# RWKV-7 recurrence into hash-routed MoE: decays of the later rounds turned on chip by VectorE, batches paired 0-2 and 1-3, and a new order of PE steps

## The chip, the cores and the metric

The kernel runs on one core of a Trainium2 chip. The metric is the device time of one execution in microseconds (us). A profile gives the span, from the first to the last instruction of one profiled execution, and the same execution's own time, which is a little longer than its span.

## What is computed

The reference is an RWKV-7 recurrence over `(batch 4, heads 8, sequence 768, head size 40)` in float32, whose output feeds a mixture of experts:

```
for t in range(S):
    y[:, :, t] = einsum('bhd,bhde->bhe', rt, state)
    Sa = einsum('bhde,bhe->bhd', state, at)
    state_decay = state * wt[:, :, None, :] - einsum('bhd,bhe->bhde', Sa, bt)
    state = state_decay + einsum('bhd,bhe->bhde', vt, kt)
x = y as (3072 tokens, 320)
out[token] = relu(x[token] @ w1[e]) @ w2[e],   e = hash of token_ids, 8 experts, F = 1024
```

## The kernel before

**Chunks, tiles, rounds.** The recurrence is computed in chunks of C = 64 steps. A tile `u` (0 to 23) is one chunk `n = u // 2` of one pair of batches `g = u % 2`: batches 0 and 1, or 2 and 3, one in partitions 0 to 63 and one in 64 to 127. The decays `w` are prepared for two chunks and all four batches at a time, in a round `ri` (0 to 5), so a round serves four tiles. A round makes `p`, which multiplies `a` (and later the output rows), and `q`, which multiplies `b` and `k`.

**Stages of a round (`decays`).** Load `w` as (batch-head, half chunk) rows; clamp (L265, VectorE); 14 chain products `prefix` and `suffix` (L270, L285; VectorE for rounds 0 and 1, GpSimd after); `own` (L275 to L277, VectorE) and, in the same step, the exchange of ends between the two halves of a chunk by eight small matmuls into `ex_ps` (L278 to L281); `ends` and the reciprocal (L290 to L300); `spread` over the rows (L304; GpSimd 2.9 us each after round 0); and then a turn from (batch-head, time) rows to (time, batch-head) rows. Round 0 turns by VectorE's transpose of 32 by 32 blocks (`turned`, L309) into borrowed space. Rounds 1 to 5 turn through DRAM: `store` (L324) scatters `p` and `q` in pieces of 40 floats, and each tile loads its slices `pl` and `ql` back (L408, L410).

**Stages of a tile.** `tile_a`: load `a`, `b`, `k` (L236, L397), multiply by `p` and `q` (L414; GpSimd after the first four tiles), turn `a` and `z = (b, k)` by TensorE (`at_t`, `z_t`), then the step `a`, a matrix of all products, of which ScalarE and VectorE copy the parts `no`, `pk` and `mk`. Four tiles make a group, whose 32 by 32 triangular blocks VectorE inverts together (`group_i`: transpose `nb`, 31 pairs of products L516 and L519, transposes `ut` and `ug`). `tile_m` completes the inverse from `ut` and `ug` (steps `x` and `u`). `tile_s` loads `r` and `v` and turns them (`rv`); `tile_b` runs the recurrence of the tile (steps `r0`, `r1`, `c`, `rcc`, `nc`, `rcv`, `s`, `y`, `sd`) and writes 128 rows of output to DRAM (`xs` L689, L692).

**What sets the order.** Every step is entered into a plan with a due time in ticks; the plan is sorted, and the engines get their instructions in exactly this order (L855 to L857). `STEPS` (L128) gives the place of a step within a tick. Tile `u` does its part of `tile_b` at tick `u + LAG`, LAG = 8. So ticks 8 to 23 hold the recurrence of one tile and `tile_a` of the tile eight later, ticks 24 to 31 the recurrence alone, and before tick 8 only `tile_a` and the first inversions run. `order` breaks ties: decays (8) and inversions (9) come behind steps of the same time. SyncE's queue issues nearly all loads and stores, in the plan's order; GpSimd's queue issues `py` and the output rows. An instruction that waits holds up everything behind it on its engine or queue.

**Buffers that the change meets.** PSUM: `psa` and `psb`, two buffers each, taken in turn. `z_all` has NZ = 11 slots. `xi`, `um`, `xs`, `py` have one buffer.

After the recurrence all its SBUF is freed, weights are loaded, and the experts run one after another (L935 on).

The changed order of steps touches these lines:

```
STEPS = ["c", "z", "rcc", "nc", "rcv", "s", "a", "y", "x", "sd", "r0", "at_t", "u", "r1", "rv"]
decays(2, -5.5, 0.45, (0.5, 2.5), 6.41, 6.43, 6.5, 6.6)
    decays(ri, t - 5.8, t - 5.3, (t - 5.2, t - 3.9), t - 3.75, t - 3.6, t - 3.55, t - 3.2)
    group_i(gi, 3.43, 3.47, 6.4)
    group_i(gi, t0 + 0.05, t0 + 0.1, t0 + 3.1)
```

Of the kernel before, what the change touches and what calls it, by code (L numbers as in the profile page):

```python
# [8 lines left out]
F32 = mybir.dt.float32  # L9
# [9 lines left out]
def kernel(  # L19
# [108 lines left out]
    STEPS = ["c", "z", "rcc", "nc", "rcv", "s", "a", "y", "x", "sd", "r0", "at_t", "u", "r1", "rv"]  # L128
# [21 lines left out]
    NZ = LAG + 3  # L150
    z_all = hold.tile([P, NZ, 2, HP, P], F32, name="z_all")
    for lo, hi, when in ((0, 4, -9.0), (4, LAG, -3.0), (LAG, NZ, 0.3)):
        @at_tick(when)
        def _(lo=lo, hi=hi):
            nc.gpsimd.memset(z_all[:, lo:hi].rearrange("p i b hp (two x) -> p (i b hp two) x", two=2)[:, :, D:C], 0.0)

    def z_r(u):
# [7 lines left out]
    lent = [x_all[:].rearrange("p i b hp x -> p (i b hp x)"),  # L165
            z_all[:, LAG:LAG + 3].rearrange("p i b hp x -> p (i b hp x)")]

    @at_tick(0.35)
    def _():
        nc.gpsimd.memset(x_all[:].rearrange("p i b hp (two x) -> p (i b hp two) x", two=2)[:, :, D:C], 0.0)  # L170
# [23 lines left out]
    pq_dram = [[nc.dram_tensor(f"{n}_rows{i}", (RN * C, B * H, D), F32) for n in "pq"] for i in range(NR)]  # L194
# [38 lines left out]
    def load(eng, dst, src, b0, t0):  # L233

        for be in range(2):
            eng.dma_start(per_head(dst[half(be)]),  # L236
                          src[b0 + be, :, t0:t0 + C, :].rearrange("h t e -> t h e"))
# [11 lines left out]
    def decays(ri, t_load, t_clamp, t_chain, t_own, t_ends, t_spread, t_store):  # L249
# [5 lines left out]
        @at_tick(t_load)  # L255
        def _():
            x["pb"] = pb = work.tile([P, HC * D], F32, tag="pb", name="pb")
            x["qb"] = work.tile([P, (HC + 1) * D], F32, tag="qb", name="qb")
            for y in range(2 * RN):
                src = w.rearrange("b h (n t) e -> (b h) n (t e)", t=HC)[:, ri * 2 * RN + y]  # L260
                eng = nc.scalar if fast and y % 2 else nc.sync
                eng.dma_start(pb[y * BH:(y + 1) * BH], src)
# [9 lines left out]
        def own():  # L272
            p, q = segs(x["pb"]), segs(x["qb"])
            x["own"] = own = work.tile([P, SEG, D], F32, tag="own", name="own", bufs=1)
            nc.vector.tensor_tensor(own[:], p[:, :, SL - 1], q[:, :, SL - 1], op=OP.mult)  # L275
            for s in range(SEG - 2, -1, -1):
                nc.vector.tensor_tensor(own[:, s], own[:, s], own[:, s + 1], op=OP.mult)  # L277
            x["ex"] = ex = bank([P, D], "ex_ps")  # L278
            for y in range(2 * RN):
                mm(ex[y * BH:(y + 1) * BH], ident[:, (y | 1) * BH:((y | 1) + 1) * BH],  # L280
                   ones[:, 0:D] if y % 2 else own[:, 0])  # L281
# [24 lines left out]
        def turned(i, src):  # L306
            lo, hi = (lent[i][:, j * BH * D:(j + 1) * BH * D] for j in range(2))
            x["qp"[i]] = lo, hi
            nc.vector.transpose(lo.rearrange("p (c e) -> p e c", e=D), src.rearrange("p (t e) -> p e t", e=D))  # L309
            nc.scalar.copy(hi[half(1)], lo[half(1)])  # L310
            if i == 0:
                nc.scalar.copy(lo[half(1)], lo[half(0)])
                nc.scalar.copy(hi[half(0)], hi[half(1)])
            else:
                lo, hi = (t.rearrange("p (g be x) -> p g be x", be=2, x=DM) for t in (lo, hi))
                nc.scalar.copy(hi[half(0), :, 1], lo[half(1), :, 0])
                nc.scalar.copy(lo[half(1), :, 0], lo[half(0), :, 1])
                for j in range(RN):
                    nc.sync.dma_start(pq_dram[ri][0][half(j)].rearrange("t bh e -> t (bh e)"), x["p"][j][half(j)])

        def store(i):
            src = (x["pb"][:], x["qb"][:, D:])[i]
            for y in range(2 * RN):
                nc.sync.dma_start(pq_dram[ri][i][y * HC:(y + 1) * HC].rearrange("t bh e -> bh t e"),  # L324
                                  src[y * BH:(y + 1) * BH].rearrange("p (t e) -> p t e", e=D))
# [6 lines left out]
        def spread_all():  # L332
            if fast:
                spread(nc.vector, x["qb"][:], x["ends"][:, 1:])
                turned(0, x["qb"][:, D:])
                recip()
                spread(nc.vector, x["pb"][:], x["own"][:])
                turned(1, x["pb"][:])
            else:
                spread(nc.gpsimd, x["pb"][:], x["own"][:])  # L340
                spread(nc.gpsimd, x["qb"][:], x["ends"][:, 1:])
# [6 lines left out]
        at_tick(t_ends, order=8)(ends_and_recip)  # L348
        at_tick(t_spread, order=8)(spread_all)
        if not fast:  # L350
            for i in range(2):
                at_tick(t_store + 0.25 * i, order=8)(lambda i=i: store(i))

        @at_tick(t_ends + 0.5, order=8)
        def _():
            p = bank([P, P], "en_ps")
            nc.tensor.transpose(p[0:R, :], e2_r(ri)[:], ident[:])
            x["pend"] = t = work.tile([P, RN, B, HP], F32, tag="pend", name="pend", bufs=5)
            for par in range(2):
                rows = half(par)  # L360
                nc.scalar.copy(t[rows].rearrange("p n b h -> p n (b h)"),
                               p[rows].rearrange("p (n y c two) -> p n y c two", n=RN, y=2, two=2)[:, :, 0, :, par])

    def of_batches(rows, b0, n):
        return rows[:, b0 * H:(b0 + n) * H, :].rearrange("t bh e -> t (bh e)")

    def tile_a(u):
# [8 lines left out]
        if early:  # L376
            t_in, t_pq, t_mul = -8.9 + 0.01 * u, None, -6.0 + 0.01 * u
            t_mulz = -6.1 + 0.01 * u if u < 2 else t_mul - 0.005
            t_z, t_at, t_a = u - 0.3, (-0.15, 0.5, 0.95, 1.0)[u], u + 0.9 if u < 3 else u + 0.4
        elif second:  # L380
            base = 4 + 0.7 * (u - 4)
            t_in, t_pq, t_mul = (0.55, 0.97, 0.2, 1.05)[u - 4], 3.1 + 0.05 * (u - 4), base - 0.5
            t_mulz = t_mul
            t_z, t_at, t_a = base - 0.3, base - 0.15, base + 0.4
        else:
            t_in, t_pq, t_mul = u - 2.3, max(u - 2.4, 6.9 + 0.02 * (u - 8)), max(u - 1.7, 7.0)
            t_mulz = t_mul
# [3 lines left out]
        def _():  # L391
            x["z"] = z_r(u)
            x["at"] = r1_r(u // GRP) if u in (3, 7) else at_r(u)
            load(eng, x["at"][:], a, 2 * g, n * C)
            for be in range(2):
                for src, rows in ((b, half(be)), (k, half(1 - be))):
                    eng.dma_start(per_head(x["z"][rows, be]),  # L397
                                  src[2 * g + be, :, n * C:(n + 1) * C, :].rearrange("h t e -> t h e"))

        if not early:  # L400
            @at_tick(t_pq)
            def _():
                pl = work.tile([P, DM], F32, tag="pl", name="pl")
                ql = work.tile([P, 2, DM], F32, tag="ql", name="ql")
                x["p"], x["q"] = pl[:], [ql[:, be] for be in range(2)]
                p_rows, q_rows = (d[rn * C:(rn + 1) * C] for d in pq_dram[ri])
                for be in range(2):
                    eng.dma_start(pl[half(be)], of_batches(p_rows, 2 * g + be, 1))  # L408
                for i in range(2):
                    eng.dma_start(ql[half(i)], of_batches(q_rows, 2 * g, 2))  # L410
# [4 lines left out]

        @at_tick(t_mulz)
        def _():
            eng = nc.vector if early else nc.gpsimd
            if early:
                q = rounds[0]["q"][rn]  # L420
                x["q"] = [q[:, (2 * g + be) * DM:(2 * g + be + 1) * DM] for be in range(2)]
            for be in range(2):
                times(eng, x["z"][:, be], x["q"][be])

        @at_tick(t_mul)
        def _():
            if early:
                p = rounds[0]["p"][rn]
                x["p"] = p[:, (2 * g + rn) * DM:(2 * g + rn + 1) * DM]
            times(nc.vector if early else nc.gpsimd, x["at"][:], x["p"])  # L430
# [25 lines left out]
        def _():  # L456
# [11 lines left out]
            x["no"] = no = work.tile([P, 2, HP, BLK], F32, tag="no", name="no", bufs=LAG)  # L468
            nc.scalar.copy(pk, pb[..., 0:BLK])
# [10 lines left out]
            nc.scalar.copy(no[:], pb[..., BLK:])  # L480

# [52 lines left out]
    def tile_m(u, t0):  # L534
# [4 lines left out]
        @at_tick(t0 - 1, "x")  # L539
# [24 lines left out]
    def tile_s(u, t0):  # L564
# [6 lines left out]
        def _():  # L571
            x["r"], x["x"] = r_r(u), x_all[:, u % 3]
            load(nc.sync, x["r"][:], r, 2 * g, n * C)
            for be in range(2):
                nc.sync.dma_start(per_head(x["x"][half(1 - be), be]),
                                  v[2 * g + be, :, n * C:(n + 1) * C, :].rearrange("h t e -> t h e"))

        @at_tick(t0 - 0.3)
        def _():
            x["py"] = py = work.tile([P, DM], F32, tag="py", name="py", bufs=1)  # L580
            for be in range(2):
                nc.gpsimd.dma_start(py[half(be)], of_batches(pq_dram[ri][0][rn * C:(rn + 1) * C], 2 * g + be, 1))
# [13 lines left out]
    def tile_b(u, t0):  # L596
# [61 lines left out]
        if not last:  # L658
            @at_tick(t0, "s")
            def _():  # L660
# [9 lines left out]
                pend = rounds[ri]["pend"][0:R, rn, 2 * g:2 * g + 2]  # L670
# [6 lines left out]
        def _():  # L677
# [12 lines left out]
            for be in range(2):  # L690
                r0 = (2 * g + be) * S + n * C
# [15 lines left out]
    decays(0, -9.0, -8.0, (-7.9, -7.6), -7.7, -7.4, -7.2, None)  # L707
    decays(1, -8.5, 0.1, (0.15, 1.85), 1.88, 2.2, 2.65, 2.7)
    decays(2, -5.5, 0.45, (0.5, 2.5), 6.41, 6.43, 6.5, 6.6)
    for ri in range(3, NR):  # L710
        t = ri * RN * NG
        decays(ri, t - 5.8, t - 5.3, (t - 5.2, t - 3.9), t - 3.75, t - 3.6, t - 3.55, t - 3.2)
# [5 lines left out]
    for gi in range(NU // GRP):  # L718
# [3 lines left out]
        else:  # L722
            group_i(gi, t0 + 0.05, t0 + 0.1, t0 + 3.1)
# [362 lines left out]
```

## Time and profile before

| | |
|---|---|
| median of 3 runs | 781.4 us (777.3 to 785.85) |
| profiled execution, its own time | 782.22 us |
| its span | 780.4 us |
| mean granted TensorE clock | 0.874 |
| TensorE busy | 623.9 us, 80% of the span |
| VectorE busy | 337.1 us, 43% |
| ScalarE busy | 278.5 us, 36% |
| GpSimd busy | 253.8 us, 33% |
| DMA packets | 201886, of them 177518 under 512 B |
| DMA traffic | 83.31 MB |

A row of instructions in the profile gives line, engine, operation, output and inputs, shape, count, then busy time and the mean of one in ns, then the engine's idle time ahead of them and what ended it. In a timeline a row begins with start and duration in us, and a bracket gives the idle time before it and the releaser. The clock is the share of full speed that TensorE was granted. `PEld` is the loading of weights into TensorE, which overlaps its matmuls.

### The profile page before, as it was taken

Reading aid. Unit: us, or ns where it says so; the run is one execution under the profiler, and the core shown is the slowest. Engines: PE = TensorE matmul, PEld = TensorE weight load, DVE = VectorE, ACT = ScalarE, POOL = GpSimd, SP = SyncE. Lnnn points to the kernel's source line nnn. Section 1 sums busy time; section 2 is a strip of 40 time slices with the busy share of each in tenths; the row PEclk is TensorE's granted clock in tenths of the full one; section 3 lists DMA queues with packets and bytes.
Section 4 is the critical chain, followed back from the end, with each engine's and each line's share of the span. In section 5 each row is a group of like instructions: output and inputs, shape, how many; then the busy total and the mean of one; then the engine's idle time right before and its main releaser. Section 6 shows DMA issues by size and latency. Waiting matters only on the chain.

```text
span 780.4 us, 24437 instructions
## 1 busy us (share of the span) xinstructions
PE 623.9 (80%) x10686; PEld 468.4 (60%) x10686; DVE 337.1 (43%) x713; ACT 278.5 (36%) x614; POOL 253.8 (33%) x336
## 2 busy tenths in 40 slices
PE   0343607899789898999989889189999999999993
PEld 0342506788668777888778778146465565565652
DVE  6849802667684656465658512111711102102100
ACT  0642502467455655665665554011101111101110
POOL 3253536525453755433323122221230212310100
PEclk9965555699886979997999999669899999999997
DMA  9567375577477659774435232696532162320000
GB/s 168 111 111 152 60 143 113 93 152 138 79 141 139 99 87 131 132 122 54 49 47 67 54 63 45 217 348 221 165 108 85 42 221 59 100 85 8 26 3 28
DMA packets 201886, 83.31 MB, mean 107 GB/s; under 512 B 177518, under 2 KB 192367, under 8 KB 201776
## 3 DMA queue, kind: packets, MB, share of 16 engines
q1 hardware_dynamic: 189008, 64.32, 38.8%
q0 software_dynamic: 6336, 16.08, 9.3%
q10 hardware_dynamic: 6432, 1.31, 1.0%
q8 instruction: 85, 1.39, 0.7%
q14 instruction: 25, 0.20, 0.1%
HBM read 66.56 MB, written 15.44 MB: 105 GB/s over the span
## 4 chain that ended last, share of the span: by engine, by line
PE 62%; issue 8%; DVE 6%; ACT 6%; DMA 3%; POOL 2%; SPq 2%; POOLq 0%; ACTq 0%; DVEq 0%
PE dn_ps L921 12%; PE up_ps L901 10%; PE r_ps L220 6%; PE s_ps L220 6%; PE y_ps L220 4%; PE rc_ps L220 4%; PE u_ps L220 3%; PE t_ps L485 3%; PE up_ps L897 3%; PE a_ps L220 3%; PE sd_ps L701 2%; PE z_ps L452 2%; PE nc_ps L654 2%; ACT rt L592 2%; DMA xg<-x_rows,src_all 1%
## 5 line engine op out<-in xcount | busy, mean ns | idle before, releaser
L921 PE MATMUL dn_ps<-w,ht 128*128 128x320 f32 x384 | 104.9, 433 | 0.0
L901 PE MATMUL up_ps<-xt,w 128*128 128x416 f32 x256 | 97.7, 536 | 0.0
L921 PEld LDWEIGHTS dn_ps<-w,ht 128*128 128x128 f32 x384 | 72.8, 190 | 32.1 <-issue 1.9
L911 POOL DMA_INDIRECT out_dram<-o,idx_all x26 | 25.7, 987 | 190.4 <-ACT o L910 185.5
L901 PEld LDWEIGHTS up_ps<-xt,w 128*128 128x128 f32 x256 | 49.2, 197 | 48.6 <-issue 48.6
L692 POOL DMA_DIRECT2D x_rows<-xs x48 | 26.3, 554 | 159.4 <-DVE xs L689 83.3
L519 DVE TENSOR_TENSOR ub<-ub,outer 128x31 f32<-128x31 f32 (+15 forms) x186 | 65.0, 349 | 6.4
L645 DVE TENSOR_TENSOR mr<-rc_ps,after 128x1024 f32<-128x1024 f32 x24 | 29.4, 1224 | 86.1 <-PE rc_ps L220 86.1
L516 DVE TENSOR_TENSOR outer<-ub,nb 128x31 f32<-128x31 f32 (+15 forms) x186 | 63.0, 338 | 4.8 <-ACT ub L501 0.2
L904 DVE TENSOR_SCALAR ht<-up_ps 128x416 f32<-128x416 f32 x32 | 18.9, 591 | 96.9 <-PE up_ps L901 96.9
L886 DVE COPY xt<-xg_ps 128x384 f32<-128x384 f32 x24 | 12.1, 552 | 101.7 <-PE xg_ps L885 101.7
L452 PE MATMUL z_ps<-ident,z_all 64*128 64x64 f32 x384 | 32.0, 277 | 29.9 <-POOL z_all L414 14.1
L452 PEld LDWEIGHTS z_ps<-ident,z_all 64*128 64x128 f32 x384 | 27.9, 180 | 33.4 <-POOL z_all L414 14.6
L414 POOL TENSOR_TENSOR z_all<-z_all,ql 128x320 f32<-128x320 f32 x40 | 33.9, 864 | 40.0 <-DMA ql<-q_rows 22.1
L910 ACT COPY o<-dn_ps 128x320 f32<-128x320 f32 x24 | 10.2, 426 | 101.6 <-PE dn_ps L921 101.6
L220 PE MATMUL rc_ps<-rt,cv 64*64 64x64 f32 x1536 | 38.1, 245 | 9.4 <-ACT cv L628 8.9
L220 PEld LDWEIGHTS rc_ps<-rt,cv 64*64 64x64 f32 x1536 | 31.1, 153 | 15.9 <-ACT cv L628 10.0
L674 ACT COPY st<-sc 40x320 f32<-40x320 f32 x44 | 20.1, 457 | 57.0 <-DVE sc L671 56.7
L906 ACT ACTIVATE ht<-up_ps 128x416 f32<-128x416 f32 x32 | 16.0, 515 | 66.3 <-PE up_ps L901 66.2
L880 POOL DMA_INDIRECT xg<-x_rows,src_all x26 | 27.2, 1044 | 30.5 <-PE xg_ps L885 15.8
L897 PE MATMUL up_ps<-xt,w 64*128 64x416 f32 x128 | 29.7, 566 | 7.1 <-DVE xt L886 3.2
L220 PE MATMUL a_ps<-at_t,z_t 64*64 64x64 f32 x1408 | 32.2, 251 | 3.6 <-ACT at_t L438 2.6
(189 smaller groups left out, 1168.0 us busy)
## 6 DMA issues: line engine op xcount, KB each, us to landing
w<-in_moe_w_dram SPq DMA_DIRECT2D x8, 1280.0 KB
w<-in_moe_w_dram SPq DMA_DIRECT2D x8, 1024.0 KB
ql<-q_rows SPq DMA_DIRECT2D x40, 160.0 KB
r<-in_r_dram SPq DMA_DIRECT2D x48, 80.0 KB
x_all<-in_v_dram SPq DMA_DIRECT2D x48, 80.0 KB
py<-p_rows POOLq DMA_DIRECT2D x48, 80.0 KB, 4.4
x_rows<-xs POOLq DMA_DIRECT2D x48, 80.0 KB, 2.6
wt<-in_w_dram SPq DMA_DIRECT2D x6, 640.0 KB
```

The source lines that it names most:

```text
L220: nc.tensor.matmul(out_, lhsT=lhsT, rhs=rhs, start=start, stop=stop, skip_group_check=True)
L414: eng.tensor_tensor(t, t, by.rearrange("p (h e) -> p h e", e=D), op=OP.mult)
L452: nc.tensor.transpose(p[:, i, c0:c0 + C], x["z"][half(i), be, hp, :], ident[half(i), half(i)])
L516: nc.vector.tensor_tensor(tv, ub[:, 0:j + 1, j:j + 1].to_broadcast([P, j + 1, m]), nb[:, j, j + 1:].unsqueeze(1).to_broadcast([P, j + 1, m ...
L519: nc.vector.tensor_tensor(o, o, tv, op=OP.add)
L645: nc.vector.tensor_tensor(t[:].rearrange("p two h t -> p (two h) t"), p[:].rearrange("p two (h t) -> p (two h) t", t=C), after[:].unsqueez ...
L692: nc.gpsimd.dma_start(x_rows[r0:r0 + C, :], xs[half(be)])
L880: nc.gpsimd.indirect_dma_start(out=xg[:, 0:DM], out_offset=None, in_=x_rows[:], in_offset=bass.IndirectOffsetOnAxis(ap=idx, axis=0))
L897: nc.tensor.matmul(banks[-1][:], lhsT=w1[rows, w:w + P], rhs=xt[rows, 2, 0:n], start=True, stop=False)
L901: nc.tensor.matmul(p[:], lhsT=w1[:, c * F + f * P:c * F + (f + 1) * P], rhs=xt[:, c, 0:n], start=False, stop=(c == 1))
L911: st = nc.gpsimd.indirect_dma_start(out=out[:], out_offset=bass.IndirectOffsetOnAxis(ap=idx, axis=0), in_=o[:], in_offset=None, bounds_che ...
L921: nc.tensor.matmul(p[:], lhsT=ht[:, f, j * P:(j + 1) * P], rhs=w2[:, f, :], start=(f == 0), stop=(f == FP - 1))
```

## The change

- Rounds 2 to 5 are turned by VectorE's transpose, `p` and `q`, into SBUF (`pt`, and `qt`, one buffer each). `p` goes to DRAM in one contiguous store for the later `py`; the upper and lower halves of `q` are put in place by three DMAs from SBUF to SBUF. Round 1 still goes through DRAM, but is loaded back for all its tiles at once. The per-tile loads `pl` and `ql` are gone; the multiplications read `pt` and `qt`.
- Batches are paired 0 with 2 and 1 with 3. With the rows of `w` loaded in another order (16 rows to a DMA), a turned round then has both batches of a pair in the right halves; `p` needs no copies between halves, in round 0 either.
- Round 2's `own`, exchange, `ends` and `spread` come at 3.38 to 3.5, ahead of the first inversion, and not at 6.41 to 6.5 behind it. Round 2 is turned at 6.45.
- In rounds 3 to 5 the exchange comes half a tick behind `own`, and the transpose `en_ps` a tick behind that.
- Step `u` goes between `c` and `rcc`; `z` goes from there to between `rcv` and `s`; `x` goes one tick earlier. Inversions are due sooner (`t0 + 2.85`, not `t0 + 3.1`, behind a step `a` that is itself 0.07 tick later).
- `b` and `k` are loaded at `u - 1.42` and multiplied at `u - 0.6` (before: `u - 2.3` and `u - 1.7`), `a` multiplied at `u - 0.9`; `z_all` has 10 slots. `no` is copied ahead of `pk`.

```diff
-    STEPS = ["c", "z", "rcc", "nc", "rcv", "s", "a", "y", "x", "sd", "r0", "at_t", "u", "r1", "rv"]
+    STEPS = ["c", "u", "rcc", "nc", "rcv", "z", "s", "a", "y", "x", "sd", "r0", "at_t", "r1", "rv"]
...
-    NZ = LAG + 3
+    NZ = LAG + 2
...
+    def batch(g, be):
+
+        return be * NG + g
...
+        def turned(i, dst):
+            src = x["qb"][:, D:] if i else x["pb"][:]
+            nc.vector.transpose(dst.rearrange("p (c e) -> p e c", e=D), src.rearrange("p (t e) -> p e t", e=D))
+
+        def turn_p():
+            x["p"] = pt = work.tile([P, BH * D], F32, tag="pt", name="pt", bufs=1)
+            if ri != 1:
+                turned(0, pt[:])
+                nc.sync.dma_start(p_dram[ri][:].rearrange("t c e -> t (c e)"), pt[:])
             else:
+                nc.sync.dma_start(pt[:], p_dram[ri][:].rearrange("t c e -> t (c e)"))
+
+        def turn_q():
+            x["q"] = qt = work.tile([P, 2, BH * D], F32, tag="qt", name="qt", bufs=1)
+            if ri == 1:
+                for i in range(2):
+                    nc.sync.dma_start(qt[half(i)], q_dram[:].rearrange("(be t) c e -> t be (c e)", be=2))
+                return
+            turned(1, qt[:, 0])
+            copy = nc.scalar.copy if fast else nc.sync.dma_start
+            copy(qt[half(1), 1], qt[half(1), 0])
+            copy(qt[half(0), 1], qt[half(1), 0])
+            copy(qt[half(1), 0], qt[half(0), 0])
...
-            t_in, t_pq, t_mul = u - 2.3, max(u - 2.4, 6.9 + 0.02 * (u - 8)), max(u - 1.7, 7.0)
-            t_mulz = t_mul
+            t_in, t_inz, t_mul, t_mulz = u - 2.3, u - 1.42, u - 0.9, u - 0.6
...
-                for be in range(2):
-                    eng.dma_start(pl[half(be)], of_batches(p_rows, 2 * g + be, 1))
-                for i in range(2):
-                    eng.dma_start(ql[half(i)], of_batches(q_rows, 2 * g, 2))
...
-        @at_tick(t0 - 1, "x")
+        @at_tick(t0 - 2, "x")
...
-    decays(2, -5.5, 0.45, (0.5, 2.5), 6.41, 6.43, 6.5, 6.6)
+    decays(2, -5.5, 0.45, (0.5, 2.5), 3.38, 3.41, 4.0, 3.5, (6.45, 6.46))
...
-        decays(ri, t - 5.8, t - 5.3, (t - 5.2, t - 3.9), t - 3.75, t - 3.6, t - 3.55, t - 3.2)
+        decays(ri, t - 5.8, t - 5.3, (t - 5.2, t - 3.9), t - 3.75, t - 3.17, t - 2.17, t - 3.1, (t - 1.57, t - 1.44))
...
-            group_i(gi, t0 + 0.05, t0 + 0.1, t0 + 3.1)
+            group_i(gi, t0 + 0.03, t0 + 0.06, t0 + 2.85)
```

In the new signature of `decays` the times are those of load, clamp, chain, `own`, exchange, `en_ps`, `spread` and the two turns.

## The prediction

> **What bounds the kernel now.** I read busy time and clock by stretch first (start and end in us, busy time of each engine, clock, DMA share, GB/s):
>
> ```profile
> 0.00:117.00 117.00, 37.22 (x779) 32.68 (x779) 76.00 (x160) 39.87 (x85) 48.18 (x67) 0.69 0.67 124
> 117.00:409.00 292.00, 259.81 (x6700) 222.35 (x6701) 175.29 (x383) 163.17 (x353) 134.52 (x183) 0.86 0.62 105
> 409.00:494.00 85.00, 75.32 (x2232) 65.52 (x2230) 37.20 (x76) 42.63 (x93) 17.22 (x33) 1.00 0.32 55
> 494.00:780.40 286.40, 251.55 (x976) 147.85 (x976) 48.58 (x96) 32.85 (x84) 53.86 (x54) 0.93 0.36 117
> ```
>
> Four stages: a prologue in which TensorE works 37 of 117 us; ticks 8 to 24, TensorE 89% busy at a clock of 0.86; the last ticks at full clock; the experts (286 us), whose instructions the change leaves alone. Next, how the prologue ends, in the timelines of TensorE, VectorE and GpSimd and the chain of what ended last:
>
> ```profile
> 117.11 0.70 PE L485 MATMUL t_ps<-ident,at 64*128 64x64 f32 x8 [21.45 <-POOL at L414]
> 132.88 0.27 PE L220 MATMUL ex_ps<-own,ident 128*32 128x40 f32 x1 [5.38 <-DVE own L277]
> ...
> 58.48 1.98 DVE L507 STREAM_TRANSPOSE nb<-pk 128x1024 f32<-128x1024 f32 x1
> 87.60 0.31 DVE L275 TENSOR_TENSOR own<-pb,qb 128x160 f32<-128x160 f32 x1
> 129.39 0.24 DVE L743 TENSOR_SCALAR eid<-tok 128x24 int32<-128x24 int32 x1 [30.42 <-DMA tok<-in_moe_token_ids_dram]
> ...
> 95.05 2.89 POOL L304 TENSOR_TENSOR pb<-pb,own 128x1280 f32<-128x1280 f32 x1
> 114.57 1.67 POOL L414 TENSOR_TENSOR z_all<-z_all,ql 128x320 f32<-128x320 f32 x2 [11.83 <-DMA ql<-q_rows]
> ...
> 111.53 2.91 DMA ql<-q_rows
> ```
>
> TensorE stands 21.45 us before the first tick: round 2's `own` comes only behind the first inversion (87.6), then `spread` (95.05), stores, loads (landed 114.4), the multiplication. Then it stands 5.38 us more, since the exchange needs round 3's `own`, which stands in VectorE's queue behind `eid`, which waits for token ids queued in SyncE's queue behind those transfers. Last, what a steady tick is made of, and what stops it:
>
> ```profile
> 442.93 0.69 PE L220 MATMUL rc_ps<-rt,cv 64*64 64x64 f32 x32 [1.08 <-ACT cv L628]
> 182.76 1.01 PE L452 MATMUL z_ps<-ident,z_all 64*128 64x64 f32 x16 [0.54 <-ACT cv L593]
> 202.00 0.27 PE L220 MATMUL ex_ps<-own,ident 128*32 128x40 f32 x1 [2.41 <-DVE own L277]
> 211.56 0.69 PE L220 MATMUL x_ps<-ut,no 32*32 32x32 f32 x32 [1.40 <-DVE ends L292]
> 227.44 1.13 PE L220 MATMUL y_ps<-z_all,mr 128*64 128x40 f32 x32 [2.39 <-DVE mr L645]
> 303.72 0.37 PE L220 MATMUL y_ps<-z_all,mr 128*64 128x40 f32 x6 [2.04 <-issue]
> ```
>
> `mr` (L645) marks the ticks: tick 8 at 134.38, tick 9 at 157.04, 10 at 171.59, 11 at 185.68, ... 24 at 408.77, 25 at 420.81. An undisturbed early tick is 14.09 us, a late one 12.05. Ticks 9 to 24 take 274.4, against 16 x 14.09 = 225.4: 49 us lie in waits of 1.4 to 2.4 us and in the lower clock after them.
>
> **The change part by part.** *Prologue.* Round 2's `own`, `ends`, reciprocal now precede the inversion: 1.95 + 0.32 + 1.15 + 0.24 = 3.7 us of VectorE (rows at 87.60 to 92.3). Against that, `a` of tile 1 stood 4 us behind round 1's exchange (3.99 idle at 44.5, for `own`) and no longer does; I let these cancel, so the inversion again ends near 87.6 (a bound from either side: 83 to 92). VectorE then turns `p` and `q`. Round 0's rows are the same instruction:
>
> ```profile
> 17.55 2.71 DVE L309 STREAM_TRANSPOSE x_all<-qb 128x1280 f32<-128x1280 f32 x1
> ```
>
> So `pt` is there at 90.3. But the tiles 4 to 7, one each 5.6 us (copies `pk` at 74.70, 80.27, 85.83, 91.97), are not faster: round 1 still goes through DRAM, its 2 x 2.9 us of `spread` for round 2 now stands between their multiplications, and GpSimd's last `mk` ends near 95.1 as now. Then its queue holds a memset and four chain products (0.2 + 4 x 0.53) and the multiplication of `a` (0.86): 98.4. TensorE's turn of tile 8's `a` moves from 117.1 to 98.4. From there to `rcv`'s end: 0.70 + 1.86 + 1.14, 1.1 of ScalarE's copies, then c 1.1, u 1.85, 1.06, 1.04, 1.06 (half-clock rows of 117 to 134) = 10.9, so 109.3. `mr` waits longer: SyncE's queue issues the `pt` store, two `q` copies, a third when they have landed (near 97), `b`, `k` and `a` of tiles 8 to 10 (10.5), `r` and `v` (2.6), then the token ids at 108, landed 2.4 later; `eid`, `mine`, three pairs, `own`: 114.4. Tick 8: 134.4 - 114.4 = **20 us gained**. The exchange half a tick behind `own` takes the 5.38 wait away; it is in these 20.
>
> *The pipeline.* `u` (1.05) now covers ScalarE's copies between `c` and `rcc`, `z` between `rcv` and `s`: the 0.54 goes, a tick becomes 13.55, and 16 of them 216.8. The price is on VectorE. In every fourth tick the order behind `mr` is `ut`, `ug`, `sc`, `pt`, `mk`, `xs` (and `qt`). From the end of `rcv`: mr 1.14, two transposes to 4.75, sc 5.2, pt 7.8, mk 8.4, xs 8.85. TensorE does z 1.0, s 1.8, a 1.1, y 1.5, x 0.6, sd 1.0, and `r0` at 7.0 must wait until `xs` has emptied the bank: 1.85, in three ticks (10, 14, 18) = 5.6. The step `x` a tick earlier takes most of the slack that `ut` had (VectorE needs 21.4 for the pairs, 2.1 for nb, 5.2 for two ticks' small work, 4.1 for own and ends, 2.3 per tick of waiting, in 37.5 us): late by 0 to 4 us, I take 2, for four groups = 8. Tick 9 starts cold, 4; routing work at tick 13 as now, 3.
>
> *The clock.* After the waits of 2.41, 2.39 and 2.04 above, the next matmuls ran at half speed for 2.7, 6.8 and 1.5 us more than their full-speed rows, mean 3.7; after the 1.40 they did not. The Trainium skill (TensorE: Matmul & The Clock Gate, HAM oscillation) allows idle gaps up to about 3.4 us, and by it the new waits of about 2 cost only themselves. By the row, four of them cost 4 x 3.7 = 15 more. Page's sum for the pipeline 237, row's 252. I take the row: the gaps here are shorter than the page's and lost the clock. 216.8 + 5.6 + 8 + 4 + 3 + 15 = 252.4 against 274.4: **22 gained**.
>
> *Late ticks.* `u` fills the 1.08 before `rcc`: 7 x 1.05 = 7.4. The last group's `sc` behind `ut` and `ug` meets a tick without z and a: x waits 5.2 - 3.3 = 1.9, with half a clock loss 1.9 more. **3.6 gained**.
>
> *Transfers.* Gone: 40 `pl`, 40 `ql` loads, 32 scattering stores of 1024 pieces (33 thousand of 202 thousand packets). New: three copies of 327 KB a round. No row shows such a copy; the nearest, the `py` loads (80 KB), land in 2.2 to 5.5. I take 5, two in sequence with 0.6 of issue each 11; bounds 5 and 20. `qt` is turned 11.5 us behind `rcv` of ticks 10, 14, 18; the copies end at 22.5, and `b`, `k` of the round's first tile, queued behind the third copy on SyncE with the next `a`, `r` and `v`, land near 24, are multiplied by 26. `z` is due at about 30 (two ticks on). So 4 us of cover; at the bound of 20 it is gone and each round stops TensorE 5 us, 3 x (5 + 3.7) = 26. Fewer packets could also end waits such as the 2.04: worth up to 10.
>
> Other edits cost nothing on the path: the earlier `no` copy (ScalarE 36% busy), the contiguous `p` store, 16-row loads of `w` (SyncE 0.45 each more, before the first clamp, under 1 us), later loads of `b` and `k` (cover above), round 0's three copies of `p` less (2.7 us of ScalarE, 1.3 on the path, left as margin).
>
> Sum on the profiled execution: span 780.4 - 20 - 22 - 3.6 = 734.8; with the 1.8 around it 736.6. That execution's 782.2 stands 0.8 above the median: I predict 736.
>
> **The rivals.**
> A, as summed: 736, own range 722 to 750.
> B, VectorE paces the ticks. For: the window of 37.5 us is already full, and routing adds 5 to 8 us in groups 1 and 2. Against: in steady ticks VectorE now waits 1 to 2 us before `mr`. Five groups late by 5, not 2, with a clock loss in some: 5 x (3 + 1.4) takes the pipeline's 22. 758.
> C, the clock holds, as the page has it: 15 less, and with fewer packets some `issue` waits gone, 8 less: 713.
> D, nothing gained, since the tiles 4 to 7 or the token ids are later than I have them (20 us more in tick 8) and B holds: 778.
> E, slower: the `q` copies. `b` and `k` stand behind the third copy in SyncE's queue, so long copies reach the round's first tile. At 15 us a copy, two in sequence are 31 in place of 11: 20 later, less the 4 of cover, with a clock loss 19.7, in four rounds 79: 815. It decides from 11 us a copy on (46 gained / 4 = 11.5 a round). For: half of the queue's loads share it, DMA share 0.6. Against: 1.28 MB of weights landed in 5.7 us at 494.66.
>
> **How the numbers follow.** Chances: A 0.47, B 0.21, C 0.15, D 0.08, E 0.09. The likeliest gives 736. From C's 713 to B's 758 with its unknowns (a late `z` adds up to 9): 710 to 767 leaves D and E out, 0.17. Within 1% of 781.4 (what this measurement can tell) is 773.6 to 789.2: D. Faster 0.83, same 0.07, slower 0.10.
>
> **What would show it.** Right: `own` of round 2 ahead of the first `nb`; the turn of tile 8's `a` near 98 without a wait above 5 us; `mr` of tick 8 near 114; late ticks at 11.0; no wait of `ex_ps` for `own`; `r0` waiting for `xs` in ticks 10, 14 and 18. Wrong: `z_ps` waiting for `z_all` in ticks 12, 16, 20 (copies late), or `y_ps` for `mr` in most ticks (B); tick 8's `mr` beyond 125 fells the prologue's sum.

## The result

| kernel | median of its runs, us | range | ratio to the kernel before (95%) |
|---|---|---|---|
| before, beside the changed kernel | 779.35 | 773.63 to 785.85 | |
| changed | 747.65 | 739.65 to 751.35 | 0.9583 (0.9459 to 0.9707) |

The change makes the kernel 4.2% faster. The profiled execution of the changed kernel took 748.57 us; its span is 746.8 (before: 782.22 and 780.4). The forecast was 736, with 722 to 750 for the likeliest case.

The span falls by 33.6 us. To see where, both traces are cut at the same three events: `mr` of tick 8, of tick 24 and of tick 31 (`mr` is L650 now). This is the view by stretches of the changed kernel: start and end, length, then busy time of TensorE, its weight loads, VectorE, ScalarE and GpSimd, the granted clock, DMA share and GB/s.

```profile
0.00:124.40 124.40, 56.93 (x1145) 49.35 (x1145) 86.55 (x175) 44.27 (x96) 56.82 (x83) 0.71 0.62 118
124.40:375.49 251.09, 233.08 (x6414) 200.63 (x6403) 183.63 (x379) 154.21 (x343) 118.68 (x149) 0.93 0.51 97
375.49:457.23 81.74, 77.87 (x2124) 67.31 (x2124) 34.37 (x74) 40.72 (x89) 12.93 (x25) 0.92 0.29 53
457.23:746.80 289.57, 254.17 (x1024) 149.73 (x1022) 50.10 (x97) 32.90 (x84) 54.00 (x54) 0.93 0.35 116
```

Before, the same four stretches took 134.38, 274.39, 82.30 and 289.33 us. So the prologue gains 10.0 (forecast 20), ticks 8 to 24 gain 23.3 (forecast 22), ticks 24 to 31 gain 0.6 (forecast 3.6), the experts nothing. The second number looks like a hit; the experiments below say otherwise. The cut at `mr` of tick 8 also does not part the same work in both kernels: `s` and `a` of tick 8 used to run behind it and now run ahead of it (119.70 to 124.60), so about 4.8 us of work have moved from the second stretch into the first.

**The prologue in the changed kernel.** First TensorE: start, duration, what it is, and in brackets how long it stood and for whom. `z_ps` here is tile 4's, `t_ps` is the turning of tile 8's `a`, the event that the forecast put at 98.4.

```profile
54.35 0.25 PE L218 MATMUL ex_ps<-own,ident 128*32 128x40 f32 x1 [4.84 <-DVE own L282]
76.70 1.62 PE L458 MATMUL z_ps<-ident,z_all 64*128 64x64 f32 x13 [21.98 <-POOL z_all L427]
84.87 1.62 PE L458 MATMUL z_ps<-ident,z_all 64*128 64x64 f32 x13 [2.66 <-POOL z_all L427]
108.49 0.70 PE L490 MATMUL t_ps<-ident,at 64*128 64x64 f32 x8
```

The wait of 21.45 us for tile 8 is gone. In its place stands one of 21.98 us for tile 4. Before, that wait was 14.10 us, and `z_ps` of tiles 4 and 5 began at 69.06 and 74.51:

```profile
69.06 1.94 PE L452 MATMUL z_ps<-ident,z_all 64*128 64x64 f32 x16 [14.10 <-POOL z_all L414]
74.51 1.60 PE L452 MATMUL z_ps<-ident,z_all 64*128 64x64 f32 x16
```

What tile 4 waits for is in the chain of work that ended last, and what then follows is in GpSimd's timeline:

```profile
62.26 4.59 DMA q_rows<-qb
67.49 8.17 DMA qt<-q_rows
77.45 2.86 POOL pb L311
80.31 2.86 POOL qb L311
```

```profile
75.78 1.67 POOL L427 TENSOR_TENSOR z_all<-z_all,qt 128x320 f32<-128x320 f32 x2 [5.69 <-DMA qt<-q_rows]
77.42 2.90 POOL L311 TENSOR_TENSOR pb<-pb,own 128x1280 f32<-128x1280 f32 x1
80.28 2.89 POOL L311 TENSOR_TENSOR qb<-qb,ends 128x1280 f32<-128x1280 f32 x1
103.64 1.28 POOL L484 TENSOR_TENSOR mk<-mk,after 128x512 f32<-128x512 f32 x1 [4.26 <-ACT mk L483]
107.45 0.86 POOL L427 TENSOR_TENSOR at<-at,pt 128x320 f32<-128x320 f32 x1
```

Round 1 still goes through DRAM, and its `q` now comes back whole (8.17 us) where it came in slices, one per tile. SyncE's timelines have the issue of these loads, first before, then changed:

```profile
64.24 1.17 SPq L410 DMA_DIRECT2D ql<-q_rows  x2
```

```profile
66.86 1.24 SPq L329 DMA_DIRECT2D qt<-q_rows  x2
```

A slice for tile 4 is made of the rows of two of the four stores, the whole is made of all four: its load is issued 2.6 us later, just when the last store has landed (62.26 + 4.59 = 66.85). Behind tile 4's products stand the two `spread` multiplications of round 2. The last `mk` ends at 104.92 (103.64 + 1.28). Before, it ended at 95.10, and there the forecast left it:

```profile
93.81 1.29 POOL L477 TENSOR_TENSOR mk<-mk,after 128x512 f32<-128x512 f32 x1 [4.76 <-ACT mk L476]
```

VectorE's timeline shows round 2's `own` ahead of the first `nb`, as foretold, the turning of `p`, and the end of the stretch:

```profile
50.52 2.98 DVE L280 TENSOR_TENSOR own<-pb,qb 128x160 f32<-128x160 f32 x1 [0.77 <-POOL pb L311]
56.89 1.96 DVE L512 STREAM_TRANSPOSE nb<-pk 128x1024 f32<-128x1024 f32 x1
94.67 2.75 DVE L315 STREAM_TRANSPOSE pt<-pb 128x1280 f32<-128x1280 f32 x1 [8.51 <-POOL r L427]
120.40 0.44 DVE L748 TENSOR_SCALAR eid<-tok 128x24 int32<-128x24 int32 x1 [8.98 <-DMA tok<-in_moe_token_ids_dram]
124.40 1.22 DVE L650 TENSOR_TENSOR mr<-rc_ps,after 128x1024 f32<-128x1024 f32 x1
```

`pt` is turned at 94.67, where the forecast had it done by 90.3. VectorE was through with the inversion at 86.15 and stood 8.51 us until tile 7's product (`r`) had read round 1's `pt`: there is only one such buffer.

The copies from `qt` to `qt` are in SyncE's timeline. The third may start when the second has landed: it waited 4.1 us, until 105.33, so that a copy takes about 4.7 us (105.33 - 100.58), against the 5 of the forecast. In the later rounds it is 4.4 to 5.3 us.

```profile
100.00 0.53 SPq L333 DMA_DIRECT2D qt<-qt  x1
100.58 0.59 SPq L334 DMA_DIRECT2D qt<-qt  x1
105.33 0.46 SPq L335 DMA_DIRECT2D qt<-qt  x1
118.16 0.62 SPq L741 DMA_DIRECT2D tok<-in_moe_token_ids_dram  x1
```

### The profile page after: what moved, and what is told of

Its sections match the earlier page's. It is cut to its first block, busy times and chain, and to the rows that moved or that the text cites. A ratio compares the mean times of both kernels' runs of the same rounds, so it can differ in the third digit from the quotient of the medians.

```text
span 746.8 us, 24358 instructions
## 1 busy us (share of the span) xinstructions
PE 622.0 (83%) x10686; PEld 467.0 (63%) x10686; DVE 354.7 (47%) x721; ACT 272.1 (36%) x611; POOL 242.4 (32%) x311
## 2 busy tenths in 40 slices
DMA packets 164158, 76.74 MB, mean 103 GB/s; under 512 B 143247, under 2 KB 155536, under 8 KB 164049
## 4 chain that ended last, share of the span: by engine, by line
PE 48%; issue 19%; DVE 12%; ACT 7%; POOL 5%; DMA 4%; SPq 3%; POOLq 0%; DVEq 0%; ACTq 0%
PE dn_ps L926 7%; PE up_ps L906 5%; PE r_ps L218 5%; PE rc_ps L218 4%; PE s_ps L218 4%; PE u_ps L218 3%; PE t_ps L490 3%; PE y_ps L218 3%; PE a_ps L218 3%; POOL xg L885 3%; PE z_ps L458 2%; PE c_ps L218 2%; PE sd_ps L706 2%; PE nc_ps L659 2%; PE up_ps L902 2%
## 5 line engine op out<-in xcount | busy, mean ns | idle before, releaser
L650 DVE TENSOR_TENSOR mr<-rc_ps,after 128x1024 f32<-128x1024 f32 x24 | 29.3, 1222 | 60.3 <-PE rc_ps L218 60.3
L427 POOL TENSOR_TENSOR z_all<-z_all,qt 128x320 f32<-128x320 f32 x40 | 33.9, 864 | 33.9 <-DMA z_all<-in_k_dram 14.7
L459 ACT COPY z_t<-z_ps 128x1024 f32<-128x1024 f32 x22 | 22.3, 1013 | 39.2 <-PE z_ps L458 39.1
```

The source lines that it names most:

```text
L427: eng.tensor_tensor(t, t, by.rearrange("p (h e) -> p h e", e=D), op=OP.mult)
L650: nc.vector.tensor_tensor(t[:].rearrange("p two h t -> p (two h) t"), p[:].rearrange("p two (h t) -> p (two h) t", t=C), after[:].unsqueez ...
```

## The experiments

Four kernels ran beside the kernel before, which took 783.75 us there (777.84 to 791.85); their ratios are to this. The changed kernel was not run again with them. Besides the median, each was read by the start of `mr` in the one trace that it left:

| | before | changed | own early | spread late | ids early | ug later |
|---|---|---|---|---|---|---|
| median, us | 779.35 | 747.65 | 769.90 | 763.99 | 754.63 | 759.67 |
| ratio to before | | 0.9583 | 0.9829 | 0.9763 | 0.9634 | 0.9663 |
| profiled span | 780.4 | 746.8 | 765.5 | 762.4 | 752.0 | 761.3 |
| tick 8 | 134.38 | 124.40 | 126.22 | 128.27 | 122.78 | 125.28 |
| ticks 8 to 24 | 274.39 | 251.09 | 267.57 | 269.99 | 261.88 | 270.08 |
| of that TensorE idle | 26.6 | 18.0 | 30.0 | 22.0 | 22.8 | 24.4 |
| clock in it | 0.88 | 0.93 | 0.93 | 0.87 | 0.92 | 0.88 |
| ticks 26 to 28 | 24.09 | 29.75 | 24.09 | 25.56 | 25.54 | 22.47 |

(Idle is the length less TensorE's busy time.) The profiled execution with `ug` later is the longest of its four, 763.16 us (the others: 751.28 to 760.29); only what it does better than the others is read from it, and the waits of single instructions. It enters no mean.

**1. The kernel before, with round 2's `own` early.** The order of round 2 alone, with its `spread` and stores, without turning on chip and with the old ticks:

```
-    decays(2, -5.5, 0.45, (0.5, 2.5), 6.41, 6.43, 6.5, 6.6)
+    decays(2, -5.5, 0.45, (0.5, 2.5), 3.38, 3.41, 3.5, 3.6)
```

> The kernel before, with only one thing of the change: own, ends and reciprocal of round 2 ahead of the first inversion (3.38 and 3.41 in place of 6.41 and 6.43), and with them its spread and stores (3.5, 3.6). Rounds are still turned through DRAM, the order of a tick is the old one. Theory 1 (the order alone gives the prologue's gain, the turning on chip gives it nothing): the 21.45 us that TensorE stands before tick 8's turning falls to about 10, mr of tick 8 comes 8 to 12 us earlier, 768 to 771, ratio 0.985 to 0.990. Theory 2 (without the turning on chip the stores and loads of round 2 keep tile 8 late, or its spread delays tiles 5 to 7 by 5.8 us): 776 to 784.

Measured: ratio 0.9829 (0.9709 to 0.9949), `mr` of tick 8 at 126.22, 8.2 us earlier than before. The numbers are near those of theory 1: 8.2 of the 10.0 us come with the order alone. But the wait for tile 8 fell to 12.63 us only, not to 10, and `spread` does delay tile 5, as theory 2 had it, by half of what it had. Its TensorE timeline (tile 4's and tile 5's `z`, tile 8's `a`):

```profile
69.48 1.94 PE L452 MATMUL z_ps<-ident,z_all 64*128 64x64 f32 x16 [8.22 <-POOL z_all L414]
77.66 1.94 PE L452 MATMUL z_ps<-ident,z_all 64*128 64x64 f32 x16 [2.67 <-POOL z_all L414]
109.18 0.70 PE L485 MATMUL t_ps<-ident,at 64*128 64x64 f32 x8 [12.63 <-POOL at L414]
```

This kernel turns tile 8's `a` at 109.18, the changed one at 108.49. Here tile 4 starts at 69.48, with round 1's `q` in slices; tile 5 follows 8.18 us later with `spread` between them, as in the changed kernel (8.17), against 5.45 before (69.06 to 74.51). Then TensorE stands 12.63 us for round 2's way through DRAM. The changed kernel saves this wait and loses 7.2 us (76.70 - 69.48) earlier on.

**2. Round 2's `spread` behind tile 7's products.**

```
-    decays(2, -5.5, 0.45, (0.5, 2.5), 3.38, 3.41, 4.0, 3.5, (6.45, 6.46))
+    decays(2, -5.5, 0.45, (0.5, 2.5), 3.38, 3.41, 4.0, 5.7, (6.45, 6.46))
```

> The changed kernel, with round 2's two multiplications on GpSimd (spread, 2 x 2.9 us) moved from behind tile 4's products to behind tile 7's. Theory (GpSimd's order is what made the prologue fall short): tiles 5 to 7 come 5.8 us earlier, the last mk before tick 8 ends near 89 in place of 95, and tile 8's a is turned near 103 to 105 in place of 108.5: mr of tick 8 near 119 to 121 (124.4 before), 742 to 745. Rival (VectorE's queue holds it): spread then ends later than the last pairs, pt and qt are turned behind it, the copies and the token ids behind them go later by as much: mr of tick 8 at 124 to 128, 747 to 751.

Measured: ratio 0.9763 (0.9654 to 0.9873), `mr` of tick 8 at 128.27, 3.9 us later than in the changed kernel. The trace is that of the rival; the time is longer than even the rival's 747 to 751, though the intervals of the two ratios overlap. TensorE, GpSimd and VectorE in its trace:

```profile
77.64 1.63 PE L458 MATMUL z_ps<-ident,z_all 64*128 64x64 f32 x13 [22.67 <-POOL z_all L427]
83.09 1.60 PE L458 MATMUL z_ps<-ident,z_all 64*128 64x64 f32 x16
107.55 0.70 PE L490 MATMUL t_ps<-ident,at 64*128 64x64 f32 x8 [0.67 <-POOL at L427]
```

```profile
94.55 2.90 POOL L311 TENSOR_TENSOR pb<-pb,own 128x1280 f32<-128x1280 f32 x1
97.39 2.95 POOL L311 TENSOR_TENSOR qb<-qb,ends 128x1280 f32<-128x1280 f32 x1
100.27 1.31 POOL L484 TENSOR_TENSOR mk<-mk,after 128x512 f32<-128x512 f32 x1
```

```profile
97.48 2.71 DVE L315 STREAM_TRANSPOSE pt<-pb 128x1280 f32<-128x1280 f32 x1 [11.04 <-POOL pb L311]
124.54 0.18 DVE L748 TENSOR_SCALAR eid<-tok 128x24 int32<-128x24 int32 x1 [14.80 <-DMA tok<-in_moe_token_ids_dram]
```

From tile 4 to tile 5 it is 5.45 us again, so `spread` in its old place costs 2.7 us and not 5.8: GpSimd had gaps between the tiles that took up half. Moved, it stands ahead of tile 6's `mk` (100.27), and the last `mk` ends at 103.24, only 1.7 us earlier than in the changed kernel. TensorE's turning of tile 8's `a` gains 0.9, and everything on VectorE's and SyncE's queues is later: `pt` at 97.48 (94.67 in the changed kernel), then the copies and the loads, and `eid`, last of them, at 124.54 (120.40).

**3. The token ids loaded in the prologue.**

```
+        yield
         iota_e = const.tile([P, E], I32)
...
     steps = routing()
+    at_tick(-3.0)(lambda: next(steps, None))
```

> The changed kernel, with the load of the token ids issued in the prologue, ahead of tick 0, in place of at tick 8; eid stays where it is in VectorE's queue. Theory (mr of tick 8 waits on VectorE behind eid, which waits for the ids): eid's idle time of 8.98 us falls to what the queue ahead leaves, own of round 3 ends by 118, mr of tick 8 follows rcv's end (118.2) at about 119.5 in place of 124.4: 4 to 5 us less, 742 to 744. Rival (y would have waited for r, v or p of the same queue anyway, or z of tile 8 is late): y starts at the same time, 746 to 749.

Measured: ratio 0.9634 (0.9517 to 0.9751), not to be told from the changed kernel's; the 742 to 744 us expected were not met (754.63). `mr` of tick 8 comes at 122.78, 1.6 us earlier; 4 to 5 were expected. The wait has only changed its owner. VectorE, then GpSimd:

```profile
111.55 0.17 DVE L749 TENSOR_SCALAR eid<-tok 128x24 int32<-128x24 int32 x1
118.78 0.36 DVE L751 TENSOR_TENSOR mine<-eid,iota_e 128x192 f32<-128x192 int32 x1 [7.06 <-POOL iota_e L744]
```

```profile
116.90 1.75 POOL L292 TENSOR_TENSOR qb<-qb 128x160 f32<-128x160 f32 x3
118.61 0.14 POOL L744 IOTA iota_e<- 128x8 int32 x1
```

`eid` runs at once at 111.55, 8.9 us earlier. The next instruction, `mine`, needs the `iota_e` of the same step, which stands on GpSimd behind round 3's chain products. And there was little to win: `z`, `s` and `a` now lie between `rcv` and `y`, and in the changed kernel `y` of tick 8 stood only 1.34 us, for `sc`, which comes behind `mr` in VectorE's queue. Here `y` starts 1.6 us earlier (125.17 against 126.78), and tick 9 is 1.2 us earlier (143.20 against 144.44).

**4. `ug` turned behind `xs`.**

```
             nc.vector.transpose(ut[:].rearrange("p g s -> p s g"), ub[:])
+
+        @at_tick(t2 + 0.26, order=9)
+        def _():
+            ub, ug = x["u"], x["ug"]
             nc.vector.transpose(ug[:].rearrange("p g t -> p t g"), ub[:].rearrange("p s t -> p t s"))
```

> The changed kernel, with the second turning of each group's inverse (ug) moved behind xs of the same tick, so that sc, pt's turning and mk stand one transposition (1 us) further forward in VectorE's queue. Theory (a wait near 2 us costs the clock): the 1.97 us that x stood for sc at tick 26 falls below 1, the two half-speed ticks behind it (17.5 and 12.3 us) come back to 11 each, some 7 us less, and up to 3 more in ticks 10, 14, 18, 22: 738 to 742, ratio 0.987 to 0.992. Rival 1 (the clock fell at tick 26 for another reason): the wait goes, the ticks stay, no more than 2 us less: 745 to 748. Rival 2 (ug is now late for u a tick on): a new wait at u, slower than the changed kernel.

Measured: ratio 0.9663 (0.9553 to 0.9772). As a whole that is no gain over the changed kernel (738 to 742 us were expected, 759.67 came), but at tick 26, where the edit aims, the theory holds. The changed kernel there (VectorE, then TensorE), and its next 10 us:

```profile
398.55 1.98 DVE L532 STREAM_TRANSPOSE ut<-ub 128x1024 f32<-128x1024 f32 x1
400.38 1.86 DVE L533 STREAM_TRANSPOSE ug<-ub 128x1024 f32<-128x1024 f32 x1
402.10 0.47 DVE L676 TENSOR_TENSOR sc<-s_ps,pend 128x320 f32<-128x320 f32 x1
```

```profile
402.62 0.69 PE L218 MATMUL x_ps<-ut,no 32*32 32x32 f32 x32 [1.97 <-DVE sc L676]
```

```profile
403.00:413.00 10.00, 10.00 (x190) 8.84 (x185) 0.99 (x3) 5.04 (x12) 1.65 (x3) 0.55 0.35 67
```

And with `ug` later:

```profile
423.89 0.69 PE L218 MATMUL x_ps<-ut,no 32*32 32x32 f32 x32 [0.28 <-DVE sc L680]
```

```profile
426.00:436.00 10.00, 9.97 (x310) 8.72 (x307) 3.39 (x4) 5.46 (x13) 1.36 (x4) 1.00 0.34 69
```

TensorE is just as busy in both 10 us, but at a clock of 0.55 it does 190 matmuls and at 1.00 it does 310. The kernels with `spread` late and with the ids early have the wait too (1.97 and 1.98), and a clock of 0.83 and 0.85 in the 10 us behind it (from 428 and from 413). From tick 26 to 28 they take 25.56 and 25.54, the changed kernel 29.75, and this one 22.47. Against these 22.47, the wait of 2 us cost 3.1, 3.1 and 7.3 us: itself, and 1.1, 1.1 and 5.3 of clock. The Trainium skill (TensorE: Matmul & The Clock Gate, HAM oscillation) has gaps cost the clock from about 3.4 us on; here a wait of 1.97 to 1.98 us was followed by a lower clock in all three profiles that have it, and in the one with 0.28 the clock stayed full, so the measurement decides. The other ticks agree. From tick 8 to tick 31 the six traces have 26 waits of TensorE of 1.5 to 2.5 us that begin at full clock. Behind 21 of them the clock is at half speed no later than 3.5 us after the wait; behind five, one of them of 2.08 us, it is not.

The edit also made a new wait, as rival 2 had it: `ug` came to stand behind routing work and `qt`'s turning, and `u` of tick 11 waited 2.11 us, a wait that the changed kernel does not have.

```profile
174.46 1.22 PE L218 MATMUL u_ps<-ug,xi 32*64 32x32 f32 x32 [2.11 <-DVE ctl L983]
```

**Not tried.** The experiments suggest a version with round 1's `q` loaded in the slices of its tiles, round 2's `spread` ahead of tile 4's products (where GpSimd idles 16 us, from 53.3 to 69.2), the ids and both iotas in the prologue, and `ug` just behind `sc`. It did not run. Neither did the changed kernel with the old tick order, or with the later rounds turned through DRAM, which would tell these two parts of the change apart, or with its copies doubled. What each would take is open.

## Why the prediction was right, and where it was not

**The prologue: the step that failed.** "The tiles 4 to 7, one each 5.6 us, are not faster ... and GpSimd's last `mk` ends near 95.1 as now." It ended at 104.92. Two terms make up the difference. Tile 4 began 7.6 us later than before (76.70 against 69.06), and `spread` added 2.7 between tiles 4 and 5 (8.17 against 5.45): 10.3, against 9.8 missed. The rest of the sum held: from the last `mk` to the turning of `a` 3.6 us (3.3 in the forecast), from there to `mr` 15.9 (16.0). The forecast saw that round 1 keeps its way through DRAM, and saw the `spread`; but it took `spread` as hidden, and did not cost the whole load at all, though `q` of round 1 loses its slices in the diff.

The late tiles hold up `mr` by a second way, which the forecast had not seen either. `mr` stands behind `eid`, the ids behind the copies of `qt`, and these behind the turning of `pt`, which waits for tile 7 to give the one buffer free (94.67; the forecast let it follow the inversion at once).

That the slices are the cause of the 7.6 rests on the row of 8.17 us and on experiment 1, which has the same early `own` and `spread`, keeps the slices and begins tile 4 at 69.48. No run changed the load alone, so this cause is argued from these rows and not isolated.

**The exchange.** The 5.38 us for round 3's `own` ahead of tick 8 is gone, as foretold. A like wait, 4.84 us for round 2's `own`, stands at 54.35, and costs nothing: TensorE has then nothing to do until tile 4 comes.

**Ticks 8 to 24: right in sum, by luck.** The forecast of 252.4 met 251.1. It counted 16 whole ticks, but `s` and `a` of tick 8 lie ahead of the cut, 4.8 us. And the kernels with `spread` late and the ids early leave these ticks as they are, while their profiles show 270.0 and 261.9 there.

What repeats over the profiles is smaller: the gain in TensorE's idle time. It is 26.6 and 30.0 us in the two kernels with the old ticks, and 18.0, 22.0 and 22.8 in three with the new ones, 7.4 less in the mean (28.3 against 20.9). The largest part is the waits of `z_ps` for ScalarE's copies, 5.9 and 6.6 us with the old order and gone with the new: this is the forecast's step from 14.09 to 13.55 us a tick, which gave 8.6 for 16 ticks. A comparison at one clock, 0.93, points the same way: the changed kernel takes 16.5 us less than experiment 1 (251.09 against 267.57), 12.0 of it idle time, and the rest, 4.5, is about the work that moved over the cut.

The terms on top of the 13.55 were not those of the forecast. `x` never waited for `ut` (8 us in the forecast; its longest waits here, 1.64 and 1.21, have other causes). `r0` did not wait for `xs` (5.6 in the forecast); it waits for ScalarE's copy `xi`, 3.8 us over five ticks, as it did before for 1.5. Still, of twelve ticks at full clock only two came near 13.55 (13.83 and 13.68); the others took 14.5 to 18.8.

The clock's term came near in size: 15 us for four waits and 4 for a cold tick 9, against at most 18 (an estimate: half of the 36 us at half speed that are listed below). It was half right in kind, for short waits did cost the clock, but others than the forecast named. One of them, and ten of the us behind it:

```profile
193.71 1.13 PE L218 MATMUL y_ps<-z_all,mr 128*64 128x40 f32 x32 [1.67 <-DVE mr L650]
200.00:210.00 10.00, 10.00 (x202) 8.94 (x203) 8.45 (x20) 5.04 (x13) 7.56 (x6) 0.53 0.43 79
```

The clock is at 0.50 three times in these ticks: from 131 to 147.5, behind waits of 1.34 and 1.21 us in tick 8; from 196 to 209, behind this one; and from 271 to 277.5, behind one of 1.71. Behind 1.64 us at 230.49 it stayed full. Which waits of this length cost the clock, and why it also falls where no wait above 1 us is seen (0.50 from 355.5 to 365 in the kernel before), no run here tells. Over the kernels of the new order it moved TensorE's busy time in this stretch from 233 to 248 us.

So the gain of 23.3 us in the profile is 8.6 of idle time and 14.7 of busy time, of which about 4.8 moved over the cut and the rest goes with the clock. What the turning on chip and the fewer packets (164158 against 201886) did for the clock or the waits in these ticks has not been told apart.

**The late ticks: right in mechanism, off in one term.** An undisturbed one fell from 12.05 to 11.00, as foretold. At tick 26 `x` waited 1.97 us for `sc` behind `ut` and `ug`, where 1.9 was forecast. The term for the clock, 1.9, came to 5.3 in this profile and to 1.1 in the two others; these 3.4 us more are about what takes the stage's 3.6 down to 0.6.

**The rivals.** E is out: no `z_ps` of ticks 8 to 24 waits for a load, and a copy takes 4.4 to 5.3 us, far from the 11 from which it would decide. B is out in the changed kernel's profile: `y` waits for `mr` once in these ticks (1.67 us, at 193.71). D named the prologue's miss (tiles 4 to 7 and the token ids late), at half its size. C, that the clock holds, is half true of the first profile, with 0.93 where it was 0.88, and not of the one with `spread` late (0.87).

## What to carry to other kernels

When a change takes a transfer off one stage, look at what it does to the grain of the transfers that stay: here, what came in slices came in one piece, the first tile waited for the last one's data, and tile 4 began 7.6 us later. When the head of a queue's wait is taken away, name the next thing that the same step needs and on which queue that stands; with the token ids loaded early, VectorE waited for an iota instead, and 1.6 us were won of the 4 to 5 expected. And a stage's forecast that meets its total is not yet right: compare it term by term, over more than one execution, and see that both cuts part the same work.

## What the runs showed of the hardware

VectorE's `own` took 0.31 us in round 3, and 2.98 us in round 2, where it began 0.07 us after a `spread` on GpSimd (50.45) and ended 0.18 after it (53.32); in experiment 1 the same happened, 2.76 us. That is the block that the Trainium skill tells of (SBUF — State Buffer, Who interferes with whom): of a VectorE instruction with two SBUF inputs, as `own` is, and a GpSimd one that reads SBUF, whichever comes second waits for the whole of the other. It was hidden here, for TensorE had nothing to do until tile 4 came; on the path it would have cost the 2.7 us by which `own` was longer.
